# Float32 weights and v for the first five tiles of a windowed attention, in front of two mixture blocks

## The chip, the core and the metric

The kernel runs on one core of a Trainium2 chip. A core has five engines with a queue each, worked through in order: TensorE (PE in the profile, with its weight loads as PEld), VectorE (DVE), ScalarE (ACT), GpSimd (POOL) and SyncE (SP), which here issues every DMA. The metric is the time of one execution on the device, in microseconds (us); lower is better. The median before is 761.0 us (three runs, 760.86 to 761.29).

## The reference

Inputs are float32 or float64; q, k and v have 4 batches, 8 heads, 576 positions and 64 elements a head. The three stages follow each other, and each works on 2304 tokens of 512 elements:

```python
scores = q @ k.T / 8 - slope[h] * abs(i - j)       # kept where 0 <= i - j < 128
attn = exp(scores - max); attn = attn / (sum(attn) + 1e-9)
x = (attn @ v)                                     # heads side by side: 2304 x 512
h = x @ w_in                                       # 512 -> 1024
solu = h * softmax(h); ln = (solu - mean) / sqrt(var + 1e-6) * g_ln
x = ln @ w_out                                     # 1024 -> 512
h = x @ w2_in                                      # 512 -> 2048
g = (a0 + a1 h + a2 h^2 + a3 h^3) / (1 + |b0||h| + |b1|h^2 + 1e-6)
out = g @ w2_out                                   # 2048 -> 512
```

## The kernel before

The tokens are cut into 18 tiles of 128. Because the window is 128 positions, a tile looks at its own keys and at those of the tile before (`nb` = 2 key blocks; tiles 0 and 9 have one). For each tile the program has these steps, each a function that adds operations to a plan: `load` (q, k and v, 256 KB each), `split_v`, `scores`, `attend`, `moe_in` (x @ w_in and the normalisation), `moe_tr` (the transposed result), and for every second tile `moe_out` (@ w_out). After the 18 tiles, `ff_in` and `ff_out` run the last block in groups of 512 tokens. That late part begins at about 340 us.

Precision is bought with splits. A float32 operand is cut into a high and a low part, and three products are added instead of one slow one. The weights of both blocks come as 8-byte numbers: `decode` turns 512 columns into float32 with one ScalarE operation and two VectorE operations (lines 485, 488, 490), and a split follows. `split_w` does this for w_in (eight blocks) and w_out (eight blocks, with `split_scaled`), and both stages of the block wait for it.

In the attention there are two forms of a tile. In a plain tile (`t < PLAIN`, line 366) the exponentials stay float32: ScalarE accumulates their sum, TensorE turns them by products with the identity (line 640), they are copied out of PSUM into `pth` and `ptl`, and `attend_plain` multiplies them by v in float32 (line 698). In all other tiles the exponentials are cut into two float16 parts (`ph` by a copy, `pl` by a subtraction, lines 647 and 648); a transposing DMA on SP's queue turns each part (line 655), two for each half of the heads; v is cut into three parts by two subtractions in `split_v` (lines 571 and 572); and `attend_parts` adds five 16-bit products for each head and key block (line 723). v's sum column gives the sum of the exponentials. Before the change only tile 0 is plain, and `split_v` starts with tile 0, since tile 1 needs tile 0's v in parts.

The order of all work is not written out by hand. Each operation has a priority: the tile's number plus an offset from the table `PR`, plus an offset per stage and engine. `Plan.order` simulates the engines with fixed durations and takes, for every engine that is free, the ready operation of the lowest priority whose buffers are free; the resulting sequence is emitted, and each engine's queue keeps it. A load is an operation of SP in that sequence, so SP too works through loads, transposes and stores in order. Buffers come from small groups of slots (`SLOTS`): six PSUM banks named bk, two q buffers, five k buffers, three v buffers, seven places for raw weights. Where an operation may go to one of several engines (`copy`, `less`), the planner chooses; `copy` from PSUM goes to ScalarE or VectorE only.

TensorE gets zero products (`idle`, line 1014) wherever the planner sees it free before the time `warm` (30 us); their result is read by nobody, and their PSUM bank is kept until then. The planner counts a TensorE operation double before `cold` (6.8 us).

Of the kernel before, what the change touches and what calls it, by code (L numbers as in the profile page):

```python
# [7 lines left out]
F32 = mybir.dt.float32  # L8
# [8 lines left out]
P = 128  # L17
# [3 lines left out]


PR = {
    "bias": -3.854, "biash": -2.053, "load": 4.13, "loadv": 3.0, "v": 1.842, "s": 1.737, "pv": 0.742,
    "win": -0.814, "wout": 0.1, "wstep": 0.43, "tr": 0.53, "mo": 2.078, "e0": 3.42, "e1": 13.032,
    "npre": 26, "plain": 1, "ln": 'dve', "alt.dve": 1500.0, "alt.act": 173.113, "alt.pool": -260.7,
    "ahead": 6.509, "warm": 30000.0, "cold": 6800.0, "last": 0.192, "scores.dve": -0.568,
    "scores.pool": 0.207, "scores.pe": -0.3, "moe_in.dve": 0.919, "attend.act": -0.027,
    "moe_out.pool": 0.104, "scores.act": 0.331, "moe_in.act": 2.226, "attend.dve": 0.049,
    "moe_tr.pe": 0.145, "moe_out.dve": 0.128, "moe_out.act": 0.44, "split_v.dve": 0.115,  # L30
    "moe_out.pe": 0.224, "weights.dve": 0.0, "weights.act": -1.021, "weights.pool": -0.155,
}


# [38 lines left out]
class Plan:  # L73
# [83 lines left out]
    def order(self):  # L157
# [22 lines left out]
        done, now = [], 0.0  # L180
        left = len(self.ops)
        dma = port = 0.0

        held = {}
        for o in self.ops:
# [30 lines left out]
        while left:  # L216
            if not events:
                stuck = [(e, [(o.n, o.pri, [b.group for b in o.allocs]) for o in ready[e]][:4]) for e in engines]
                raise RuntimeError(f"no order: {stuck}")
            now = events[0][0]  # L220
            if self.kept is not None and now >= PR["warm"]:
                self.kept.left -= 1
                if self.kept.slot is not None and not self.kept.left:
                    free[self.kept.slot] = True
                self.kept = None
            while events and events[0][0] <= now:
                _, _, what, o = heapq.heappop(events)
                if what == "ready":
                    for a in o.alts:
                        ready[a[0]].append(o)  # L230
                elif what == "end":
                    for r in {self.where[b.group] for b in o.bufs}:
                        held[r] -= 1
                    for b in o.bufs:
                        b.left -= 1
                        last[b.slot][o.lag and "dma" or o.eng] = now
                        if not b.left:
                            free[b.slot] = True
                            for d in (3.0, 97.0, 127.0, 145.0, 155.0, 200.0, 270.0):
                                heapq.heappush(events, (now + d, seq, "wake", o))  # L240
                                seq += 1
            moved = True
            while moved:
                moved = False
                for e in engines:
                    if busy[e] > now:
                        continue
                    best = None
                    for o in ready[e]:
                        if (best is None or (o.pri, o.n) < (best.pri, best.n)) and fits(o, e) and (  # L250
                                o.alts[0][0] == e or sooner(o, e)):
                            best = o
                    if best is None:
                        if e != "pe" or now >= PR["warm"] or not self.idle:
                            continue
                        best = self.idle(now)
                        if not fits(best, e):
                            continue
                        ready[e].append(best)
                        left += 1  # L260
                        users[best] = ()
                        for r in {self.where[b.group] for b in best.bufs}:
                            held[r] = held.get(r, 0) + 1
                    o = best
                    if e == "pe" and now < PR["cold"] and o.n < len(self.ops):
                        o.alts = tuple((e, 2 * ns, *x) for e, ns, *x in o.alts)
                    for a in o.alts:
                        ready[a[0]].remove(o)
                        if a[0] == e:
                            o.eng, o.ns, o.fn, o.port = a  # L270
                    o.allocs = [b for b in o.bufs if b.slot is None]
                    for b in o.allocs:
                        at[b.group] += 1
                        for s, make in self.groups[b.group]:
                            if clear(s, e):
                                free[s] = False
                                last[s] = {}
                                b.slot, b.make = s, make
                                break
                    o.start = now  # L280
                    if o.lag:
                        busy[e] = now + 460.0
                        dma = max(dma, now + 1100.0) + o.ns
                        o.end = dma + o.lag
                    else:
                        at_port = max(now, port) if o.port else now
                        busy[e] = o.end = at_port + o.ns
                        if o.port:
                            port = o.end
                    done.append(o)  # L290
                    left -= 1
                    moved = True
                    heapq.heappush(events, (o.end, seq, "end", o))
                    seq += 1
                    if busy[e] < o.end:
                        heapq.heappush(events, (busy[e], seq, "free", o))
                        seq += 1
                    for u in users.get(o, ()):
                        wait[u] -= 1
                        if not wait[u]:  # L300
                            t = max(d.end + self.hop(d, u) for d in u.deps)
                            heapq.heappush(events, (max(t, now), seq, "ready", u))
                            seq += 1
# [10 lines left out]
def t_pe(n, cols, wide=True):  # L314

    return n * (cols * 0.4167 + ((17.0 if cols > 256 else 13.3) if wide else 4.0))


def t_act(n, psum=False, ptrs=0):
    return n * 0.833 + (52.0 if psum else 94.0) + 93.0 * ptrs  # L320
# [16 lines left out]
def kernel(  # L337
# [64 lines left out]
    for where, tab in SLOTS.items():  # L402
# [12 lines left out]

    nc.scalar.preload_act_table_set("natural_log_exp_and_others")
    ident = const.tile([P, P], F32, name="ident")
    nc.gpsimd.memset(ident, 0.0)
    nc.gpsimd.affine_select(
        out=ident, in_=ident, compare_op=ALU.not_equal, fill=1.0, base=0,  # L420
        pattern=[[-1, P]], channel_multiplier=1,
    )
    gsb = const.tile([P, KF], F32, name="gsb")
    acoef = const.tile([P, 4], F32, name="acoef")
    bcoef = const.tile([P, 2], F32, name="bcoef")
# [68 lines left out]
    def split(x, xa, ha, la, hk, lk, n, pri, first="pool"):  # L494
        copy(ha, xa, n, [x], [hk], pri)
        less(la, xa, lambda: ha().bitcast(F32), n, [x, hk], [lk], pri, first=first)

    def split_scaled(x, ha, la, hk, lk, g, pri):
# [4 lines left out]
            out=la(), in0=x.t, scalar=g(), in1=ha().bitcast(F32), op0=ALU.mult, op1=ALU.subtract),  # L503
            r=["gsb", x, hk], w=[lk], pri=pri, port=True)

    def split_w(g, pri):
        raw = Buf("wraw", [P, 512, 2], I32)
        x = Buf("wx", [P, 512], F32)
        if g < 2 * KD:
            n, kk = divmod(g, KD)  # L510
            cols = slice(n * 512, n * 512 + 512)
            src = w_in.rearrange("(k p) (f w) -> p k f w", p=P, w=2)[:, kk, cols]
        else:
            f = g - 2 * KD
            src = w_out.rearrange("(k p) (f w) -> p k f w", p=P, w=2)[:, f]
        plan.op("sp", t_dma(P * 4096, 4096), lambda: nc.sync.dma_start(out=raw.t, in_=src),
                w=[raw], pri=pri, lag=LAG)
        decode(x, lambda: x.t, raw, lambda: raw.t, 512, pri)
        if g < 2 * KD:
            split(x, lambda: x.t, lambda: wih[:, kk, cols], lambda: wil[:, kk, cols], ("wih", kk, n),  # L520
                  ("wil", kk, n), 512, pri, first="dve")
        else:
            split_scaled(x, lambda: woh[:, f], lambda: wol[:, f], ("woh", f), ("wol", f),
                         lambda: gsb[:, f:f + 1], pri)


    q_f, k_f, v_f, v_t, pt, ssum, xs = {}, {}, {}, {}, {}, {}, {}
# [483 lines left out]
    b.left = 1  # L1011

    def idle(now):
        return plan.filler("pe", t_pe(1, 256) * (2 if now < PR["cold"] else 1), lambda: nc.tensor.matmul(  # L1014
            b[:, 0:256], still[:, 0:P], still, start=True, stop=True), b)

    plan.idle, plan.kept = idle, b
# [38 lines left out]
```

## Time and profile before

| what | us |
|---|---|
| median of 3 runs | 761.0 |
| the profiled execution, its own time | 762.12 |
| its span, first to last instruction | 760.3 |
| TensorE busy | 738.5 (97%) |
| VectorE busy | 603.3 (79%) |
| ScalarE busy | 480.1 (63%) |
| GpSimd busy | 330.3 (43%) |

The profile is of one execution. Busy time is a sum over instructions; a matmul's record includes its way through the array, so matmuls overlap and TensorE's busy time counts the union. A row of the chain of waits has a start, a length and what the time went to: the chain is followed back from the last event, and a piece of TensorE work on it is as long as the engine needed to get on. For back-to-back matmuls the chain's lengths are therefore the price of one, and the records' own durations are not.

### The profile page before, as it was taken

How to read it: one execution, taken by the hardware profiler on the slowest of the kernel's cores; microseconds unless marked ns; L12 is line 12 of the kernel's file. 1: busy time of each engine (PE TensorE's matmuls, PEld its weight loads, DVE VectorE, ACT ScalarE, POOL GpSimd, SP SyncE). 2: the span in 40 equal slices, each digit the busy share in tenths (PEclk: the TensorE clock that was granted, in tenths of full speed). 3: DMA queues.
4: the chain of work that ended last, by engine and by line, in shares of the span. 5: the costliest groups of instructions: out<-in, count | busy, mean ns of one | idle time of the engine just before them, and what ended most of it. 6: DMA issues, size and time to landing. Idle time of an engine off the chain costs nothing.

```text
span 760.3 us, 14468 instructions
## 1 busy us (share of the span) xinstructions
PE 738.5 (97%) x5369; PEld 631.8 (83%) x5369; DVE 603.3 (79%) x1279; ACT 480.1 (63%) x922; POOL 330.3 (43%) x330
## 2 busy tenths in 40 slices
PE   8968999999999999999999999999999999999997
PEld 7857899898898999989788888888888888888885
DVE  5998987888889757555799988878877788778983
ACT  8666565666576554355887775556765667567782
POOL 5435744443444625036995743334333343323331
PEclk9969999999999999999999999999999999999999
DMA  9996997999998917054541230000100001000010
GB/s 315 276 226 108 194 263 188 238 275 249 245 258 186 177 50 120 28 183 163 160 118 56 84 104 1 1 0 22 56 1 1 1 0 56 0 2 1 1 56 28
DMA packets 123670, 85.36 MB, mean 112 GB/s; under 512 B 74448, under 2 KB 106192, under 8 KB 123600
## 3 DMA queue, kind: packets, MB, share of 16 engines
q1 hardware_dynamic: 123600, 84.44, 43.5%
q8 instruction: 42, 0.69, 0.4%
q14 instruction: 28, 0.23, 0.1%
HBM read 50.86 MB, written 16.25 MB: 88 GB/s over the span
## 4 chain that ended last, share of the span: by engine, by line
PE 85%; DVE 6%; ACT 3%; DMA 3%; issue 2%; SPq 0%; POOL 0%; DVEq 0%; ACTq 0%; POOLq 0%
PE bk L896 23%; PE h L953 14%; PE bk L818 12%; PE h L743 12%; PE bk L953 11%; PE bk L723 4%; PE bk L602 4%; PE bk L578 3%; PE bk L1014 2%; DMA dx<-w2i 1%; DVE bk L930 1%; DMA qn<-in_q_dram 1%; DVE bk L919 1%; DMA pth<-ph 1%; DVE s L617 1%
## 5 line engine op out<-in xcount | busy, mean ns | idle before, releaser
L896 PE MATMUL bk<-yh,wb 128*128 128x512 f32 (+1 forms) x540 | 132.5, 371 | 0.2 <-DVE tcc L928 0.2
L896 PEld LDWEIGHTS bk<-yh,wb 128*128 128x128 f32 x540 | 96.8, 188 | 21.2 <-DVE tcc L928 0.4
L469 POOL TENSOR_TENSOR gl<-tcc,gh 128x512 fp32r<-128x512 f32 x60 | 78.7, 1312 | 75.7 <-ACT gh L457 41.2
L916 ACT ACTIVATE bk<-bk,bcoef 128x512 f32<-128x512 f32 (+1 forms) x80 | 49.5, 618 | 88.5 <-PE bk L896 87.3
L896 PE MATMUL bk<-yh,wa 128*128 128x512 f32 (+1 forms) x420 | 101.8, 371 | 2.0 <-ACT wa L457 0.9
L919 DVE SCALAR_TENSOR_TENSOR bk<-tb,nb,bk 128x512 f32<-128x512 f32 (+1 forms) x80 | 55.9, 699 | 44.6 <-ACT tb L918 43.1
L896 PEld LDWEIGHTS bk<-yh,wa 128*128 128x128 f32 x420 | 75.4, 188 | 18.4 <-DVE tcc L928 1.9
L953 PE MATMUL h<-wo,gh 128*128 128x512 f32 x276 | 84.4, 393 | 0.6 <-ACT gh L457 0.4
L818 PE MATMUL bk<-lh,woh 128*128 128x256 f32 x288 | 84.3, 293 | 0.2 <-DVE ll L801 0.2
L818 PE MATMUL bk<-ll,woh 128*128 128x256 f32 x288 | 81.4, 283 | 0.0
L818 PE MATMUL bk<-lh,wol 128*128 128x256 f32 x288 | 81.4, 283 | 0.0
L469 POOL TENSOR_TENSOR pl<-s,ph 128x512 f16<-128x512 f32 (+1 forms) x58 | 70.1, 1220 | 17.1 <-ACT ph L457 16.1
L953 PE MATMUL bk<-wo,gh 128*128 128x512 f32 x240 | 75.1, 394 | 0.0
L459 POOL TENSOR_SCALAR gh<-tcc 128x512 fp32r<-128x512 f32 (+1 forms) x43 | 26.8, 622 | 106.8 <-DVE tcc L934 105.7
L624 ACT ACTIVATE s<-s,nm 128x256 f32<-128x256 f32 (+1 forms) x144 | 61.9, 487 | 13.3 <-DVE nm L617 13.1
L930 DVE SCALAR_TENSOR_TENSOR bk<-bk,qc,tb 128x512 f32<-128x512 f32 (+1 forms) x80 | 56.3, 704 | 7.3 <-ACT tb L923 5.4
L921 ACT ACTIVATE tb<-bk,qc 128x512 f32<-128x512 f32 (+1 forms) x80 | 51.8, 647 | 14.6 <-DVE bk L919 14.1
L953 PEld LDWEIGHTS h<-wo,gh 128*128 128x128 f32 x276 | 50.7, 188 | 11.5 <-POOL gh L459 0.6
L459 POOL TENSOR_SCALAR ph<-s 128x512 f16<-128x512 f32 (+1 forms) x32 | 20.9, 659 | 90.6 <-DMA pth<-ph 39.1
L924 ACT ACTIVATE tcc<-bk,acoef 128x512 f32<-128x512 f32 (+1 forms) x80 | 59.4, 743 | 0.0
L617 DVE CUSTOM_DVE_ANT_0 s<-bk,bias 128x256 f32<-128x256 f32 (+1 forms) x144 | 51.0, 402 | 9.2 <-PE bk L602 6.1
L928 DVE SCALAR_TENSOR_TENSOR tcc<-tcc,acoef,bk 128x512 f32<-128x512 f32 (+1 forms) x80 | 55.4, 692 | 2.3
(166 smaller groups left out, 1920.9 us busy)
## 6 DMA issues: line engine op xcount, KB each, us to landing
rw<-in_moe_w_in_dram SPq DMA_DIRECT2D x17, 512.0 KB, 4.9
rw<-in_moe_w_out_dram SPq DMA_DIRECT2D x15, 512.0 KB, 5.3
kn<-in_k_dram SPq DMA_DIRECT2D x18, 256.0 KB, 4.9
qn<-in_q_dram SPq DMA_DIRECT2D x18, 256.0 KB, 3.9
vv<-in_v_dram SPq DMA_DIRECT2D x18, 256.0 KB, 5.2
yT<-ys SPq DMA_DIRECT2D x18, 256.0 KB, 2.9
yr<-yT SPq DMA_DIRECT2D x16, 256.0 KB, 3.6
w2i<-dc SPq DMA_DIRECT2D x14, 256.0 KB, 3.4
```

What stands on the lines that cost most here:

```text
L469: "pool": (t_pool(n), lambda: nc.gpsimd.tensor_tensor(out(), a(), b(), op), True),
L617: nc.vector.tensor_tensor_reduce(out=s[:, jj, 0:W], in0=sc[r][:, jj, 0:W], in1=bs, scale=-scale, scalar=3e38, op0=ALU.add, op1=ALU.min, ac ...
L624: nc.scalar.activation(out=s[:, jj, 0:W], in_=s[:, jj, 0:W], func=ACTF.Exp, scale=-1.0, bias=nm[:, h:h + 1], accum_out=sm[:, h:h + 1] if p ...
L743: nc.tensor.matmul(h[:, cols], a[:, kk], w[:, kk, cols], start=(i == 0 and kk == 0), stop=(i == 2 and kk == KD - 1))
L818: nc.tensor.matmul(y[:, r], w[:, f, cols], x[:, f % 4], start=(f == 0 and n == 0), stop=(f == KF - 1 and n == 2))
L896: nc.tensor.matmul(h(), w[:, a, kk], y[:, b, kk, 0:n], start=(i == 0 and kk == 0), stop=(i == 2 and kk == KD - 1))
L919: o("dve", t_dve(n) + 60, lambda: stt(out=A(), in0=R(), scalar=nb1, in1=A(), op0=ALU.mult, op1=ALU.subtract), [bR], [bA])
L921: o("act", t_act(n, True, ptrs=1), lambda: act(out=R(), in_=A(), func=ACTF.Ln, scale=-1.0, bias=qc), [bA], [bR])
L924: o("act", t_act(n, True, 2), lambda: act(out=C(), in_=h(), func=ACTF.Identity, scale=acoef[:, 3:4], bias=acoef[:, 2:3]), [hb, "coef"], [bC])
L928: o("dve", t_dve(n) + 60, lambda: stt(out=C(), in0=C(), scalar=acoef[:, 1:2], in1=h(), op0=ALU.add, op1=ALU.mult), [hb], [bC])
L930: o("dve", t_dve(n) + 60, lambda: stt(out=A(), in0=A(), scalar=qc, in1=R(), op0=ALU.subtract, op1=ALU.mult), [bR], [bA])
L953: nc.tensor.matmul(acc[g][s][2](), a(slice(s * P, (s + 1) * P)), w[:, c], start=(f == 0 and i == 0), stop=(f == KF2 - 1 and i == 2))
```

## The change

`PLAIN` becomes 5, so tiles 0 to 4 are plain: no float16 parts, no transposing DMAs, no split of v for tiles 0 to 3, but sums on ScalarE, turns on TensorE, copies out of PSUM and float32 products. The first block of w_in (`pein` = 1) gets its low part from TensorE: a product with the identity, minus a product of the high part, and a copy out of PSUM. (`peout` = 0: the same for w_out is written but not used.) A constant `minus` is made on VectorE at the start. Zero products are planned until 60 us and no longer counted double. The planner takes TensorE to be slow for 6.8 us after any wait of over 3 us, by a factor of 1.85. Most priorities change a little: among others v is loaded earlier (4.28 tiles ahead, 3.0 before), q and k later (3.432, 4.13 before), and 28 blocks of the last stage's weights, not 26, are decoded ahead into DRAM.

```diff
-    "npre": 26, "plain": 1, "ln": 'dve', ...
+    "npre": 28, "plain": 5, "ln": 'dve', ...
-    "ahead": 6.509, "warm": 30000.0, "cold": 6800.0, "last": 0.192, ...
+    "ahead": 6.6, "warm": 60000.0, "cold": 6800.0, "pein": 1, "peout": 0, "last": 0.169,
...
+        slow = PR["cold"]
...
-                    if e == "pe" and now < PR["cold"] and o.n < len(self.ops):
-                        o.alts = tuple((e, 2 * ns, *x) for e, ns, *x in o.alts)
+                    if e == "pe":
+                        if now - busy[e] > 3000.0:
+                            slow = now + PR["cold"]
+                        if now < slow and o.n < len(self.ops):
+                            o.alts = tuple((e, 1.85 * ns, *x) for e, ns, *x in o.alts)
...
+    minus = const.tile([P, P], F32R, name="minus")
...
+    nc.vector.tensor_scalar(minus, ident, -1.0, None, ALU.mult)
...
+    def lower(x, w, ha, la, hk, lk, r, pri):
+
+        d = Buf("bk", [P, 512], F32)
+
+        def mm():
+            nc.tensor.matmul(d.t, w(), x.t, start=True, stop=False)
+            nc.tensor.matmul(d.t, minus, ha(), start=False, stop=True)
+        plan.op("pe", 1085.0, mm, r=[x, hk] + r, w=[d], pri=pri)
+        copy(la, lambda: d.t, 512, [d], [lk], pri, psum=True)
...
+            if g < PR["pein"]:
+                copy(part[0], lambda: x.t, 512, [x], [part[2]], pri)
+                lower(x, lambda: ident, *part, [], pri)
+            else:
+                split(x, lambda: x.t, *part, 512, pri, first="dve")
...
-        return plan.filler("pe", t_pe(1, 256) * (2 if now < PR["cold"] else 1), lambda: nc.tensor.matmul(
+        return plan.filler("pe", t_pe(1, 256), lambda: nc.tensor.matmul(
```

## Rows read from the trace of the kernel before

**Rows 1.** By stage: stretch, length, busy us per engine, clock, DMA share, GB/s.
```profile
0.00:34.00 34.00, 30.67 (x309) 26.13 (x309) 25.22 (x77) 23.18 (x58) 18.10 (x23) 0.95 0.93 288
34.00:60.00 26.00, 19.16 (x131) 15.03 (x132) 24.61 (x61) 16.54 (x33) 7.46 (x8) 0.74 0.86 221
60.00:83.00 23.00, 19.89 (x278) 17.05 (x276) 19.66 (x69) 16.81 (x36) 14.18 (x14) 1.00 0.89 162
83.00:340.00 257.00, 255.48 (x2729) 232.24 (x2725) 197.20 (x564) 147.20 (x311) 106.59 (x103) 1.00 0.80 186
340.00:740.00 400.00, 397.97 (x1860) 328.81 (x1860) 329.32 (x497) 270.49 (x473) 181.60 (x181) 1.00 0.13 44
740.00:760.30 20.30, 15.37 (x75) 12.58 (x73) 7.30 (x17) 5.83 (x15) 2.36 (x4) 0.97 0.07 26
```

**Rows 2.** Groups of TensorE instructions: count, busy us, mean ns, idle before.
```profile
L1014 PE MATMUL bk<-still 128*128 128x256 bf16 x145 | 18.7, 292 | 1.1 <-DVE still L429 1.1
```

**Rows 3.** The chain of waits, 4 to 16 us: start, length, work.
```profile
7.64 1.83 PE bk L602 x16
9.47 1.47 PE bk L640 x6
...
11.87 1.09 PE bk L602 x16
12.96 1.03 PE bk L698 x8
...
14.10 0.84 PE bk L698 x8
```

**Rows 4.** The chain of waits, 86 to 125 us.
```profile
87.35 5.50 PE h L743 x24
...
97.04 1.31 PE bk L578 x12
```

**Rows 5.** The same table by stage, for 8 to 11 us.
```profile
8.00:11.00 3.00, 3.00 (x23) 2.64 (x21) 1.47 (x8) 2.02 (x10) 2.50 (x3) 0.50 1.09 376
```

**Rows 6.** The chain of waits, 24 to 62 us.
```profile
31.68 1.34 PE bk L723 x40
...
34.18 1.19 PE h L743 x4
...
50.68 2.04 PE bk L602 x14
...
54.45 6.11 PE h L743 x16
```

**Rows 7.** SP's queue in order of time: start, length, DMA issued.
```profile
37.08 4.01 SPq L655 DMA_TRANSPOSE ptl<-pl  x1
```

**Rows 8.** VectorE in order of time: start, length, operation [idle before].
```profile
11.61 1.51 DVE L468 TENSOR_TENSOR v<-v1r 128x512 bf16<-128x512 f32 x1 [0.70 <-POOL v1r L469]
...
14.48 2.23 DVE L488 TENSOR_SCALAR dc<-dc 128x512 int32<-128x512 int32 x2
...
26.93 0.41 DVE L488 TENSOR_SCALAR dc<-dc 128x512 int32<-128x512 int32 x1
...
30.26 1.46 DVE L468 TENSOR_TENSOR wil<-dc,wih 128x512 fp32r<-128x512 f32 x1
31.64 0.68 DVE L701 TENSOR_TENSOR xr<-bk,st 128x512 f32<-128x512 f32 x1
```

**Rows 9.** GpSimd in order of time, 8 to 90 us.
```profile
13.98 2.45 POOL L469 TENSOR_TENSOR pl<-s,ph 128x512 f16<-128x512 f32 x2
```

**Rows 10.** Groups of ScalarE instructions, 0 to 60 us.
```profile
L624 ACT ACTIVATION_READ_ACCUMULATOR s<-s,nm 128x1 f32 x8 | 1.5, 187 | 0.0
...
L457 ACT ACTIVATE xh<-bk 128x512 fp32r<-128x512 f32 x2 | 1.2, 597 | 3.7 <-PE bk L578 3.7
```

**Rows 11.** The same table by stage, for 10 to 60 us.
```profile
10.00:60.00 50.00, 42.60 (x390) 35.60 (x389) 46.97 (x113) 32.70 (x65) 22.26 (x21) 0.85 0.92 262
```

**Rows 12.** TensorE in order of time, 4 to 16 us.
```profile
4.87 1.16 PE L602 MATMUL bk<-kn,qn 64*128 64x128 f32 x16
```

More of the change, by code (lines that the diff above doesn't have):

```diff
@@ L23 @@
 PR = {
[L24 to L31, printed above, removed]
+    "bias": -3.938, "biash": -2.341, "load": 3.432, "loadv": 4.28, "v": 1.842, "s": 1.737, "pv": 0.742,
+    "win": -0.911, "wout": 0.1, "wstep": 0.43, "tr": -0.387, "mo": 2.066, "e0": 3.613, "e1": 12.889,
+    "npre": 28, "plain": 5, "ln": 'dve', "alt.dve": 1500.0, "alt.act": 173.113, "alt.pool": -260.7,
+    "ahead": 6.6, "warm": 60000.0, "cold": 6800.0, "pein": 1, "peout": 0, "last": 0.169,
+    "scores.dve": -0.59, "scores.pool": 0.107, "scores.pe": -0.3, "moe_in.dve": 0.919,
+    "attend.act": -0.139, "moe_out.pool": 0.132, "scores.act": 0.331, "moe_in.act": 2.097,
+    "attend.dve": 0.165, "moe_tr.pe": -0.433, "moe_out.dve": -0.69, "moe_out.act": -0.295,
+    "split_v.dve": 0.115, "moe_out.pe": 0.224, "weights.dve": 0.16, "weights.act": -0.915,
+    "weights.pool": -0.155,
 }
@@ L417 @@
     ident = const.tile([P, P], F32, name="ident")
+    minus = const.tile([P, P], F32R, name="minus")
+    diag = const.tile([P, PR["peout"], P], F32, name="diag") if PR["peout"] else None
     nc.gpsimd.memset(ident, 0.0)
@@ L519, in split_w @@
         if g < 2 * KD:
-            split(x, lambda: x.t, lambda: wih[:, kk, cols], lambda: wil[:, kk, cols], ("wih", kk, n),
-                  ("wil", kk, n), 512, pri, first="dve")
-        else:
-            split_scaled(x, lambda: woh[:, f], lambda: wol[:, f], ("woh", f), ("wol", f),
-                         lambda: gsb[:, f:f + 1], pri)
+            part = (lambda: wih[:, kk, cols], lambda: wil[:, kk, cols], ("wih", kk, n), ("wil", kk, n))
+            if g < PR["pein"]:
[3 more added lines that the diff above has]
+                split(x, lambda: x.t, *part, 512, pri, first="dve")
+        else:
+            part = (lambda: woh[:, f], lambda: wol[:, f], ("woh", f), ("wol", f))
+            gain = lambda: gsb[:, f:f + 1]
+            if f < PR["peout"]:
+                plan.op("pool", 250, lambda: nc.gpsimd.tensor_scalar(
+                    diag[:, f], ident, gain(), None, ALU.mult), r=["gsb"], w=[("diag", f)], pri=PR["bias"] + 0.01 * f)
+                plan.op("act", t_act(512, ptrs=1), lambda: nc.scalar.activation(
+                    out=part[0](), in_=x.t, func=ACTF.Identity, scale=gain()), r=["gsb", x], w=[part[2]], pri=pri)
+                lower(x, lambda: diag[:, f], *part, [("diag", f)], pri)
+            else:
+                split_scaled(x, *part, gain, pri)
     q_f, k_f, v_f, v_t, pt, ssum, xs = {}, {}, {}, {}, {}, {}, {}
```

## The prediction, before the result was known

> **What bounds the kernel now.** I read the busy table by stage first. TensorE is busy all the time from 83 us to 740 us (255.5 of 257 us, then 398.0 of 400) at a granted clock of 1.00; before 83 us it is not, and VectorE is the full one there (24.6 of 26 us in 34 to 60) [rows 1]. So the kernel is a TensorE-bound run behind a start in which TensorE waits for VectorE. The end moves only if the start loses less TensorE time, or if TensorE gets more or less to do. I therefore keep an account of TensorE's lost time:
>
> - Idle: 3.3 + 6.8 + 3.1 = 13.3 us before 83 us, and 1.5 + 2.0 + 4.9 = 8.5 us after it [rows 1].
> - Zero products of line 1014, which only fill waits: 18.7 us, all early [rows 2].
> - Work at the lower clock. Tile 1's first scores took 1.83 us where 1.09 is the price, and six turns took 1.47 where 6 x 0.109 = 0.65 is (1.31 us for 12) [rows 3, 4]. The clock granted in 8 to 11 us was 0.50 [rows 5]. After the hole at 45 us, 14 score products took 2.04 us instead of 14 x 0.068 = 0.95 and 16 moe products 6.11 instead of 16 x 0.229 = 3.67 (5.50 us for 24) [rows 4, 6]. Together 0.74 + 0.82 + 1.09 + 2.44 = 5.1 us.
>
> Early loss: 13.3 + 18.7 + 5.1 = 37.1 us. Real work at full clock: 760.3 - 37.1 - 8.5 = 714.7 us. The change must be weighed as added work against early loss removed.
>
> **What is added on TensorE.** Tiles 1 to 4 change their kind; tile 0 was plain already, so its rows are the prices. Its eight float32 products of weights and v took 1.03 + 0.84 = 1.87 us [rows 3], or 0.234 each; a tile with two key blocks has 16 of them, 3.74 us. Turning its weights takes 16 transposes of 128x128 at 0.109 us [rows 4], 1.75 us. Removed are the two halves of 40 16-bit products, 1.34 us each [rows 6], 2.68 us. Net 3.74 + 1.75 - 2.68 = 2.81 us a tile, 11.2 us for four. The low part of the first w_in block ("lower") is one float32 and one float32r product of 512 columns. The float32r one costs 0.23 us; no row has the float32 one at 512 columns, so I bound it by two float32r products (0.46 us) and by 4 x 2 x 0.109 = 0.87 us from the turns; its gain on VectorE is one subtraction. I take the upper end, 1.0 to 1.1 us in all, and use 1.0. Sum: 12.2 us of new work.
>
> **What is removed elsewhere.** (a) Sixteen transposing DMAs (four a tile) leave SP's queue. One of them occupied it for 4.01 us, from 37.1 us on [rows 7], with all later loads behind it; tile 1's second half waited for that landing. (b) Sixteen subtractions of low weight halves and eight that split v go, most of them GpSimd's, a few VectorE's. One of VectorE's, 1.51 us at 11.6 us, stood in front of tile 1's second scores [rows 8]. (c) VectorE runs slower beside GpSimd: two integer shifts took 2.23 us beside two GpSimd subtractions (2.45 us) where one takes 0.41 alone, and a subtraction of 512 elements 1.46 us where a product of that size took 0.68 [rows 8, 9]. With (b), that stretch goes too: 1.4 + 0.8 us in these two places, and 1.5 for the moved v split, 3.7 us that I can name before tile 0's output is scaled at 31.64 us [rows 8].
>
> **What is added elsewhere.** ScalarE takes four copies of a turned 512-element block per tile (0.60 us each) and eight accumulator reads (0.187 us each, partly overlapped), and loses up to four 0.6 us copies of the high weights that GpSimd shared: +1.5 to +3.9 us a tile, 6 to 16 us for four [rows 10]. It was busy 32.7 us of 50 in 10 to 60 us [rows 11], so 39 to 48. That hides it at the low end only; I take 8, since tiles 3 and 4 finish late in that stretch. VectorE's new constant ("minus") waits at the start for GpSimd's identity and holds back the zero products' operand: 0 to 0.5 us of an interval in which nothing real runs; I take 0. The first v load moves ahead of the first k and q: 0 to 0.6 us; I take 0.1 and let the start stay 4.9 us, where the first scores begin now [rows 12]. The buffers of v are now held until the next tile's products; the third stays in its slot for about one tile: 0 to 1 us, taken at 0, because v 3 is not needed before tile 3. The fill block keeps one of six PSUM banks until 60 us of planned time and not 30: 0 to 3 us, taken at 1 inside the waits below. Two more early w2 decodes and the new priorities after 83 us lie under a full TensorE: -1 to +1 us, taken at 0. Fewer or more zero products cost nothing where TensorE would wait; one in the way costs its 0.11 us.
>
> **The new loss.** First products: 4.9 us in. The first moe products began at 34.2 us [rows 6], 2.5 us behind the scaling at 31.64. With 3.7 us named and some more from shifts and loads further on, I put them at 29 us (bounds 24 and 34). Until then TensorE has these to do: tile 0 (0.6 scores, 0.9 turns, 1.9 products, 0.4), tile 1 (2.2 + 1.75 + 3.74 + 0.4), tile 2's scores and turns (4.0) and the low part (1.0): 16.9 us in the 24.1 us from 4.9 to 29, a loss of 7.2. After that the old kernel lost 6.8 + 3.1 us idle from 34 us and 3.5 at the low clock. The second moe block came only at 54.45 us [rows 6]: between the two lay the DMA landing, the hole and the low clock. Those causes are removed, but VectorE still has the w_out decoding; I keep a third, 4.4 us, and 0.4 for the early clock. New loss: 4.9 + 7.2 + 4.4 + 0.4 = 16.9 us.
>
> Span: 714.7 + 12.2 + 8.5 + 16.9 = 752.3 us. The profiled execution took 762.12 us, 1.8 over its span; the median shown is 761.0, 0.7 over this span, so I forecast 753.0 us on the scale of the medians.
>
> **A rule against it.** Twelve turns in a row at 97 us ran at 0.109 us each, amid a stretch with a granted clock of 1.00 [rows 1, 4]; but the six turns at 9.5 us ran inside a stretch at 0.50 [rows 3, 5]. The change brings 64 more turns into the start. The Trainium skill (TensorE: Matmul & The Clock Gate, Part 4: PE-mode transpose) says that transposes do not count as activity for the full clock, which would speak against the change. The late row disagrees for short bursts among other products; the early row cannot tell turns from the wait before them. As a mechanism of this kernel it is the fourth rival.
>
> **The rivals.**
> 1. ScalarE takes VectorE's place (ends slower). Each turned block must be copied out by ScalarE before a product can start; at its upper bound (48 of 50 us) the start stays as long as now. Tiles 1 and 2 and the low part still fit where the zero products are, but tiles 3 and 4 fall behind the point at which TensorE is full: 2 x 2.81 = 5.6 us, so 761.0 + 5.6 = 766.6. It decides once ScalarE is over 95% busy between 10 and 50 us. For it: its sum; against it: 17 us free now.
> 2. A wash. The early loss falls by no more than the 12.2 us of work that is put in, to 24.9: 761.0. So it would be if the new work only replaces zero products, and moe starts at 34 us as now. For it: the 18.7 us of fill; against it: the DMA and GpSimd waits that go.
> 3. A deep gain. Moe starts at 24 us and nothing waits after it: loss 4.9 + 2.2 + 0.4 = 7.5 us, 743.6. For it: TensorE has more than enough ready once tile 1 is plain; against it: eight w_in decodes on VectorE must be done first.
> 4. Low clock from 5 to 29 us: 16.9 us of work take as much again, less the 7.2 free: +9.7, 762.7.
>
> **How the numbers follow.** Forecast (loss 11 to 23 us, 747 to 759): 0.63. Rival 1: 0.09. Rival 2: 0.10 (0.02 faster, 0.07 same, 0.01 slower). Rival 3: 0.14. Rival 4: 0.04. So faster by over 0.2% (under 759.5, about what a measurement of this kernel can tell from no change) 0.63 + 0.14 + 0.02 = 0.79, within it 0.07, slower 0.01 + 0.09 + 0.04 = 0.14. The range goes from 746, leaving out most of rival 3, to 761.5, taking in rival 2 and leaving out the two slower ones.
>
> **What would show it.** Right: first moe products before 31 us and the second block before 45; no granted clock under 0.9 in 15 to 80 us; fill plus idle before 83 us near 17 us; TensorE full from about 45 us; VectorE's shifts at 0.41 us. Float32 products at 0.117 us an instruction, turns at 0.11. Wrong: moe starting at 34 us (rival 2), ScalarE full (rival 1), turns at 0.25 us (rival 4), or a loss after 83 us well over 8.5 us, which would mean that the new order pays elsewhere.

## The result

The changed kernel takes 751.5 us (median of four runs, 750.94 to 753.49) where the kernel before took 761.1 beside it: a ratio of 0.987 (95% interval 0.985 to 0.990). The forecast was 753.0 us in a range of 746 to 761.5. The profiled execution has a span of 749.1 us.

The table by stage, which answers to [rows 1], has the same columns.

```profile
0.00:34.00 34.00, 32.19 (x288) 26.91 (x288) 23.67 (x89) 26.93 (x80) 9.55 (x16) 1.00 0.89 294
34.00:60.00 26.00, 26.00 (x208) 22.97 (x208) 24.53 (x63) 23.92 (x65) 5.33 (x4) 1.00 0.50 163
60.00:83.00 23.00, 23.00 (x209) 20.82 (x210) 21.53 (x70) 17.28 (x37) 12.46 (x13) 1.00 0.63 147
83.00:340.00 257.00, 256.28 (x2648) 231.95 (x2647) 190.70 (x548) 147.20 (x307) 100.80 (x99) 1.00 0.78 193
340.00:740.00 400.00, 398.16 (x1843) 328.73 (x1842) 331.05 (x499) 268.76 (x474) 169.72 (x171) 1.00 0.11 36
740.00:749.10 9.10, 3.92 (x18) 2.88 (x16) 0.69 (x1) 0.60 (x1) 0.00 (x0) 1.00 0.15 58
```

TensorE was idle for 13.3 us before 83 us; now it is idle for 1.8, nearly all of it before its first instruction. The granted clock, 0.95 and 0.74 in the first two stages before, is 1.00 in all rows. (That column does not show the very start: in 1.7 to 4 us, 11 zero products took 2.2 us, in 6 to 8 us, 20 took 2.0, both with a clock of 1.00.) After 83 us the picture is as it was. ScalarE is the engine that changed most: 26.9 and 23.9 us in the first two stages, 23.2 and 16.5 before; GpSimd's work there falls from 18.1 and 7.5 to 9.6 and 5.3.

The chain of waits shows what fills the start. It answers to [rows 6] and [rows 4], with line 773 for 743, 728 for 698, 670 for 640 and 753 for 723.

```profile
24.84 0.93 PE h L773 x4
...
27.76 1.93 PE bk L728 x16
...
35.19 1.14 PE h L773 x4
...
39.50 1.73 PE bk L728 x16
...
43.08 0.44 PE bk L670 x4
...
51.71 5.75 PE h L773 x24
57.46 1.75 PE bk L670 x16
```

Tile 0's moe products come in two halves now, the second from 35.2 to 39 us, since the second half of w_in is decoded late. The second tile's start only at 51.7 us; it was 54.45 us [rows 6]. In between stand the turns and the attention products of tiles 2 and 3 and the scores of tile 4 (tile 1's products came before, tile 4's come at 62.8 and 71.4 us): that is what replaced waits, zero products and slow work.

```profile
65.40 5.53 PE h L773 x24
...
75.06 1.34 PE bk L753 x40
...
79.36 5.50 PE h L773 x24
...
96.95 5.50 PE h L773 x24
```

The third tile's moe products begin at 65.15 us in the order of time; they began at 72.84. The fourth tile's begin at 79.4 us, those of the fifth at 96.95; 87.35 us was the fourth's start before [rows 4]. So 8 us of the 11.2 us between the two profiled spans are there at 79 us; of the rest 0.8 us is less idle time after 83 us [rows 1], and what remains is work that stands earlier now.

### The profile page after: what moved, and what is told of

It reads as the page before. It is cut to its first block, busy times and chain, and to the rows that moved or that the text cites. A ratio compares the mean times of both kernels' runs of the same rounds, so it can differ in the third digit from the quotient of the medians.

```text
span 749.1 us, 14112 instructions
## 1 busy us (share of the span) xinstructions
PE 739.6 (99%) x5205; PEld 634.3 (85%) x5205; DVE 592.2 (79%) x1266; ACT 484.7 (65%) x960; POOL 297.9 (40%) x302
## 4 chain that ended last, share of the span: by engine, by line
PE 89%; DVE 5%; ACT 4%; DMA 1%; issue 1%; SPq 0%; POOL 0%; POOLq 0%; DVEq 0%
PE bk L926 24%; PE h L983 14%; PE h L773 13%; PE bk L848 13%; PE bk L983 11%; PE bk L632 4%; PE bk L753 4%; PE bk L608 3%; PE bk L1044 1%; PE bk L728 1%; ACT s L654 1%; DMA dx<-w2i 1%; DVE bk L960 1%; PE bk L670 1%; DVE bk L949 1%
## 5 line engine op out<-in xcount | busy, mean ns | idle before, releaser
L926 PEld LDWEIGHTS bk<-yh,wa 128*128 128x128 f32 x420 | 75.4, 188 | 18.1 <-DVE tcc L958 1.9
L654 ACT ACTIVATE s<-s,nm 128x256 f32<-128x256 f32 (+1 forms) x144 | 63.9, 488 | 14.3 <-DVE nm L647 14.0
L467 POOL TENSOR_SCALAR gh<-tcc 128x512 fp32r<-128x512 f32 (+1 forms) x39 | 24.2, 622 | 105.2 <-DVE tcc L964 104.5
L951 ACT ACTIVATE tb<-bk,qc 128x512 f32<-128x512 f32 (+1 forms) x80 | 51.7, 647 | 12.6 <-DVE bk L949 12.0
L647 DVE CUSTOM_DVE_ANT_0 s<-bk,bias 128x256 f32<-128x256 f32 (+1 forms) x144 | 51.0, 404 | 10.5 <-PE bk L632 8.8
L958 DVE SCALAR_TENSOR_TENSOR tcc<-tcc,acoef,bk 128x512 f32<-128x512 f32 (+1 forms) x80 | 55.4, 692 | 2.1
L964 DVE SCALAR_TENSOR_TENSOR tcc<-tcc,acoef,bk 128x512 f32<-128x512 f32 (+1 forms) x80 | 55.4, 693 | 2.1
L848 PEld LDWEIGHTS bk<-lh,woh 128*128 128x128 f32 x288 | 55.0, 191 | 1.1
```

Source lines behind the costliest of these rows:

```text
L654: nc.scalar.activation(out=s[:, jj, 0:W], in_=s[:, jj, 0:W], func=ACTF.Exp, scale=-1.0, bias=nm[:, h:h + 1], accum_out=sm[:, h:h + 1] if p ...
L848: nc.tensor.matmul(y[:, r], w[:, f, cols], x[:, f % 4], start=(f == 0 and n == 0), stop=(f == KF - 1 and n == 2))
L926: nc.tensor.matmul(h(), w[:, a, kk], y[:, b, kk, 0:n], start=(i == 0 and kk == 0), stop=(i == 2 and kk == KD - 1))
L951: o("act", t_act(n, True, ptrs=1), lambda: act(out=R(), in_=A(), func=ACTF.Ln, scale=-1.0, bias=qc), [bA], [bR])
L958: o("dve", t_dve(n) + 60, lambda: stt(out=C(), in0=C(), scalar=acoef[:, 1:2], in1=h(), op0=ALU.add, op1=ALU.mult), [hb], [bC])
L964: o("dve", t_dve(n) + 60, lambda: stt(out=C(), in0=C(), scalar=acoef[:, 0:1], in1=A(), op0=ALU.add, op1=ALU.mult), [bA], [bC])
```

## The experiments

Each group of four ran on one chip beside the kernel before, in five rounds. The time is the median; the ratio is to the kernel before on that chip, with its 95% interval. Between groups I compare ratios: 0.001 is 0.76 us.

**One plain tile.** The change without its main part.

```diff
-    "npre": 28, "plain": 5,
+    "npre": 28, "plain": 1,
```

> The changed kernel with one plain tile instead of five; the zero products until 60 us, the new priorities, the low part of one w_in block on TensorE and everything else stay. Theory (the plain tiles are what pays, since they take float16 parts, splits of v and transposing DMAs out of the start): the gain of 9.6 us goes, 758 to 764 us, first moe products after 29 us, idle before 83 us above 6 us. Rival (the new order and the longer zero products pay, and the plain tiles are only carried along): 755 us or less, since 11 us of added TensorE work go too.

764.5 us, ratio 1.004 (1.003 to 1.005): slower than before by a little, and some 13 us slower than with five. The rival falls. TensorE issues 285 zero products where the changed kernel issues 106, and the second moe block comes 7 us later. The account closes: 179 zero products more (some 19.5 us) and 5.5 us more idle time, against some 10.5 us less work, make 14.5 of the 15.2 us between the profiled spans. The sign of 6 us of idle time before 83 us failed: it was 4.0, since zero products stand in the waits. These are a group's row (count, busy us, mean ns) and two rows of TensorE in order of time:

```profile
L1044 PE MATMUL bk<-still 128*128 128x256 bf16 x285 | 36.2, 284 | 1.8 <-DVE still L437 1.8
```

```profile
30.36 1.16 PE L773 MATMUL h<-wih,xh 128*128 128x512 f32 x4
...
58.66 2.11 PE L773 MATMUL h<-wih,xh 128*128 128x512 f32 x8
```

**Five plain tiles in the kernel before.**

```diff
-    "npre": 26, "plain": 1,
+    "npre": 26, "plain": 5,
```

> The kernel before with five plain tiles and nothing else changed: old priorities, zero products until 30 us, no low part on TensorE. Theory (plain tiles pay by themselves): 750 to 756 us, first moe products before 28 us. Rival (the order and the longer zero products pay): 759 us or more, since 11 us of TensorE work are added.

758.5 us, ratio 0.994 (0.991 to 0.996), with runs from 753.2 to 760.1. That lies between the two: plain tiles pay by themselves, but the median is over the theory's 756. The profiled run, near the low end, shows what is missing. Its first moe products start at 25.3 us, and 34 to 60 us has 24.7 us of TensorE work; but ahead of tile 3's moe products the chain runs into VectorE, which decodes weights (line 490) between the steps that free tile 2's moe result (lines 751 and 758):

```profile
71.10 0.45 PE bk L578 x4
...
72.81 1.21 DVE st L751
74.03 1.39 DVE dc L490
...
76.46 0.59 DVE dc L490
...
78.93 6.18 PE h L743 x19
```

TensorE's table there (stretch, length, busy us per engine, granted clock):

```profile
72.00:78.00 6.00, 2.40 (x35) 2.04 (x32) 5.80 (x7) 3.10 (x6) 3.71 (x4) 1.00 0.85 179
78.00:83.00 5.00, 4.43 (x15) 3.35 (x14) 5.00 (x21) 3.20 (x6) 0.54 (x1) 0.66 1.42 290
```

One hole of some 3.6 us and the low clock behind it: as I read it, the old priorities place VectorE's decoding badly for a start that has become shorter.

**The changed kernel with fewer zero products,** in the same order of real work.

```diff
+            zeros.append(1)
+            if len(zeros) <= 41:
+                nc.tensor.matmul(b[:, 0:256], still[:, 0:P], still, start=True, stop=True)
```

> The changed kernel in the same order of all real work, but of its 106 zero products only the first 41 (before the first scores) are issued; the 65 later ones are left out. Theory (zero products only fill waits that ScalarE and VectorE make, 65 x 0.11 = 7.1 us of them): the time stays at 751 to 752 us, TensorE is idle some 7 us more, and the granted clock stays at 1.00 because the holes are short. Rival (the zero products hold the clock up, and the longer warm stretch is part of the gain): the granted clock falls to 0.5 somewhere between 9 and 45 us and the time rises to 754 us or more.

750.8 us, 0.985 (0.983 to 0.987), the span 749.0. Without 65 zero products the time does not rise and the clock stays up, though 64 more turns than before the change run in this start. They only fill waits.

```profile
0.00:34.00 34.00, 30.52 (x242) 23.65 (x242) 22.49 (x85) 25.61 (x77) 9.04 (x16) 1.00 0.90 304
34.00:60.00 26.00, 24.48 (x192) 21.55 (x190) 24.84 (x67) 24.11 (x66) 5.60 (x5) 1.00 0.47 150
```

**Thirteen fewer of the opening ones,** the same edit with `not 28 < len(zeros) <= 41`.

> The changed kernel in the same order, but 13 of the 41 zero products ahead of the first scores are left out. The 41 took TensorE from 1.76 to 7.96 us, at 0.151 us each. If they stand in the way of scores whose q and k have landed, the scores begin 1 us or more earlier, ScalarE's full stretch begins earlier with them, and the time falls by about 1 us, to 750.5 us. Rival (q and k land at about 8 us anyway, or the clock comes up later without them): no change, or up to 1 us more.

751.3 us, 0.986 (0.984 to 0.988): no change that can be told. The 28 took 0.20 us each, the 41 of the kernel above 0.18, since the first of them run slowly, and not equally long in every execution (the changed kernel's 41 took 6.2 us in its profiled run, these 7.5). So the scores came 0.6 us before the changed kernel's 7.89, and 1.9 before those of the run above, whose span is 1.4 us shorter all the same: the times of these runs do not tell what a later first product costs. (Two traces further down show one that was kept.) TensorE in order of time, first with 28, then with 41:

```profile
1.77 5.64 PE L1049 MATMUL bk<-still 128*128 128x256 bf16 x28 [1.77 <-DVE still L437]
7.33 1.16 PE L632 MATMUL bk<-kn,qn 64*128 64x128 f32 x16
```

```profile
1.77 7.52 PE L1049 MATMUL bk<-still 128*128 128x256 bf16 x41 [1.77 <-DVE still L437]
9.21 1.16 PE L632 MATMUL bk<-kn,qn 64*128 64x128 f32 x16
```

**Three plain tiles** (`"plain": 3`).

> The changed kernel with three plain tiles. Theory (each plain tile takes waits out of the start, and the four together moved the time from 764.5 to 751.5 us): tiles 3 and 4 pay too, so 754 to 760 us. Rival (tiles 3 and 4 lie where TensorE is full, as it is from about 10 us on, and only cost their 2.7 us each): 746 to 750 us.

759.5 us, 0.997 (0.996 to 0.999): with tiles 3 and 4 in parts the kernel is 8 us slower. TensorE is busy 19.5 us of 23 in 60 to 83 us, at a clock of 0.85, and waits there for VectorE (1.8 and 1.1 us) and GpSimd (0.5); a transposing DMA costs 0.8 us after 83 us. As an account: 53 zero products more than with five (some 5.8 us), 6.0 us more idle time (4.2 of it before 83 us) and the lower clock, against some 5.3 us less work. Holes of this kind also come with other changes of the order (below), so how much of the 8 us the two tiles are worth by themselves is not shown.

```profile
L1044 PE MATMUL bk<-still 128*128 128x256 bf16 x159 | 22.3, 291 | 1.8 <-DVE still L437 1.8
```

**Seven plain tiles** (`"plain": 7`):

> The changed kernel with seven plain tiles. Theory (plain pays only while TensorE has waits to fill, and tiles 5 and 6 come after 60 us, where it has none): 2 x 2.7 us more, 755 to 759 us. Rival (every tile without splits and transposing DMAs frees more than it costs): 751 us or less.

757.0 us, 0.995 (0.994 to 0.996): 5.5 us more than with five by the medians, 5.7 by the ratios, 2.8 a tile. The start is the same, zero products and idle time too (107 against 106, 9.8 us in all against 9.5), so no new hole is in the comparison: work is added where TensorE is full.

```profile
L1044 PE MATMUL bk<-still 128*128 128x256 bf16 x107 | 16.5, 292 | 1.8 <-DVE still L437 1.8
```

**High copies on GpSimd,** to relieve ScalarE.

```diff
-                split(x, lambda: x.t, *part, 512, pri, first="dve")
+                copy(part[0], lambda: x.t, 512, [x], [part[2]], pri, first="pool")
+                less(part[1], lambda: x.t, lambda: part[0]().bitcast(F32), 512, [x, part[2]], [part[3]], pri, first="dve")
```

> The changed kernel with GpSimd, not ScalarE, as first choice for the high copies of seven w_in blocks; four of eight were ScalarE's, 0.6 us each. Theory (ScalarE, busy 38.1 us of 40 between 10 and 50 us, is what now holds the start): 2 us less, 749 to 750 us. Rival (VectorE holds it just as much, and slows beside GpSimd): 751 to 755 us.

755.9 us, 0.992 (0.990 to 0.993). As slow as the rival said and a little more, but not for its reason: the start is as full as before, and the loss lies after 83 us, in one wait of the last block's first products for GpSimd (a table row, and a row of TensorE's waits: total us, times, longest):

```profile
34.00:60.00 26.00, 26.00 (x218) 22.98 (x218) 23.71 (x67) 24.88 (x68) 6.55 (x6) 1.00 0.48 155
...
83.00:340.00 257.00, 252.60 (x2611) 229.08 (x2611) 194.93 (x559) 146.04 (x305) 101.00 (x98) 0.99 0.75 191
```

```profile
PE bk L927 <- POOL wa L467: 3.3, 1, 3.3
```

So this run does not tell whether ScalarE or VectorE holds the start.

**The old loads' order** and **no low part on TensorE.**

```diff
-    "load": 3.432, "loadv": 4.28,
+    "load": 4.13, "loadv": 3.0,
```

> The changed kernel with the old priorities of the loads (k and q 4.13 tiles ahead, v 3.0). Theory (the loads' order is not what pays): 750 to 754 us; the first scores come near 5 us and not at 7.9, and the w_in loads about 1.4 us later. Rival (the five plain tiles alone gave 758.5 us because of the old loads): 756 us or more.

758.3 us, 0.995 (0.994 to 0.996), which the theory missed. The first scores came at 7.2, not near 5, since the zero products are in front of them; the start is full, and again one hole follows, ahead of the third moe block:

```profile
60.00:83.00 23.00, 19.28 (x180) 16.80 (x177) 21.80 (x64) 15.23 (x31) 11.98 (x11) 0.94 0.72 166
```

```profile
PE h L773 <- DVE st L798: 3.5, 1, 3.5
```

The other is `"pein": 0`:

> The changed kernel without the low part of the first w_in block on TensorE: one subtraction more on VectorE (0.7 us), a copy less on ScalarE (0.6 us), 1.1 us less TensorE work. Theory (it is a small term): 750.5 to 752.5 us. Rival (it frees VectorE where the first moe products wait for it): 753 us or more, and those products start 0.7 us or more after 21.7 us.

756.3 us, 0.992 (0.990 to 0.993). Both signs of the rival are there: the first moe products start 1.1 us later. But 34 to 83 us stays full of TensorE work (49.0 of 49), and the time is lost after 83 us: 252.9 us busy of 257, with waits for GpSimd and ScalarE at the last block's weights. So the reason is neither's. Each such edit makes the planner write another order, and by the ratios another order cost 3 to 6 us here, in one or two holes.

**30 products of zeros added,** to the kernel with 41 zero products, at 18 us or at 68 us (there the same loop stands in tile 2's moe products), without any change of order. The edit for 18 us:

```diff
             nc.tensor.matmul(d.t, w(), x.t, start=True, stop=False)
+            for _ in range(30):
+                nc.tensor.matmul(d[:, 0:256], still[:, 0:P], still, start=False, stop=False)
```

> The changed kernel's order with only the first 41 zero products (that kernel took 750.8 us), and 30 products of zeros, 3.3 us of TensorE time, added to the sum of the low part at about 18 us. Theory (there TensorE waits for ScalarE and VectorE, so work put on it is hidden): 750.3 to 752 us. Rival (TensorE bounds the start as well, and the added float32 products are paid in full and only outweighed): 753.5 us or more.

> The same kernel with the 30 products of zeros added to tile 2's moe products at about 68 us instead. Theory (from about 60 us on TensorE is what everything waits for): 3.0 to 3.6 us more than with 41 zero products alone, 754 us. Rival (later waits still take some of it up): 752.5 us or less.

Early: 752.1 us, 0.988 (0.986 to 0.989), an interval that overlaps that of the kernel without them (0.983 to 0.987); 1.9 us more by the ratios, 0.8 less by the profiled spans. Late: 753.3 us, 0.990 (0.989 to 0.992), clear of it: 3.8 us more by the ratios, 1.9 by the spans, for 3.3 us of work. The late half of the theory stands. For the early half the times leave it open, but the traces say more, one execution each, as the three kernels have one order. The first scores came at 9.21 us without the 30 products, at 7.71 and 7.66 in these two, because the opening zero products happened to run faster. These are the starts of the third tile's moe products, without, early and late:

```profile
65.85 2.08 PE L773 MATMUL h<-wih,xh 128*128 128x512 f32 x8
```

```profile
64.99 2.07 PE L775 MATMUL h<-wih,xh 128*128 128x512 f32 x8
```

```profile
64.17 2.07 PE L773 MATMUL h<-wih,xh 128*128 128x512 f32 x8
```

In the late run nothing is added up to there, and it is 1.7 us ahead: the earlier opening of 1.55 us is kept in full. In the early run 0.9 of 1.5 us is left, so the 30 products had cost 0.6 us of their 3.3 by then. The fifth tile's moe products start at 97.38, 96.51 and 98.99 us: the early ones still cost 0.6 us, the late ones now 3.3, all of it. So in these executions most of the early work is hidden. The early run's profiled execution is the fastest of its four, though (750.1 us; the others 752.1 to 752.4), and what the others lost no trace shows.

**Zero products until 60 us in the kernel before** (`"warm": 60000.0`).

> The kernel before with zero products until 60 us of planned time instead of 30, nothing else. Theory (they only fill waits; they can at most keep the clock up over the hole at 45 us, whose slow work cost 3.5 us): 757 to 761 us. Rival (the fill is what pays): 754 us or less.

766.9 us, 1.009 (1.007 to 1.011): outside what either side expected. The clock is at 1.00 through the start, 61 zero products stand where the hole was, and the second moe block starts at 54.6 us, as before. So the low clock alone was not what delayed it (though this, too, is another order). The loss lies in new holes: 4.5 us of idle time in 60 to 83 us and 5.2 in 83 to 340.

```profile
34.00:60.00 26.00, 25.35 (x215) 20.90 (x215) 24.81 (x65) 19.04 (x39) 8.47 (x8) 1.00 0.86 213
```

```profile
42.06 6.76 PE bk L1014 x61
...
54.64 5.79 PE h L743 x24
```

## Why the prediction was right

**Added work.** Right. A half's eight products (16 instructions) took 1.73 us in most cases (1.93 at 27.8 us) and four turns 0.44: 3.46 + 1.75 us a tile against 2.46 to 2.68 of parts, so 2.5 to 2.75 (predicted 2.81). The low part took 1.1 us from 17.6 to 18.7 us, the upper end chosen for the float32 product.

```profile
1.76 6.20 PE L1044 MATMUL bk<-still 128*128 128x256 bf16 x41 [1.76 <-DVE still L437]
7.89 1.16 PE L632 MATMUL bk<-kn,qn 64*128 64x128 f32 x16
...
17.60 1.02 PE L519 MATMUL bk<-dc,ident 128*128 128x512 f32 x2
18.06 0.80 PE L520 MATMUL bk<-wih,minus 128*128 128x512 f32 x1
...
21.66 1.18 PE L773 MATMUL h<-wih,xh 128*128 128x512 f32 x4
```

One price in the prediction's list of what TensorE can do meanwhile was too low: tile 0's scores are 16 instructions at 0.068 us, 1.1 us and not 0.6. The account closes: opening zero products 6.2 us, 65 others at 0.11 us 7.15, idle 1.8 + 7.7, so real work is 749.1 - 22.9 = 726.2 us; predicted were 714.7 + 12.2 = 726.9.

**Early loss.** 1.8 + 13.4 = 15.2 us against 16.9, near partly by luck. The first scores came at 7.9, not 4.9 us: I had passed over what the new price of a zero product does, 41 of them ahead of the scores, slow at first. So the opening cost 8.0 us where the sum has 4.9. Between it and the first moe products 28 zero products took 3.1 us where the sum has 7.2; the 37 behind them took 4.1, where it has 4.4. The two large errors cancel. Of the low clock nothing is left but the slow opening.

**Where the gain arises.** The first moe products came at 21.7 us, under my bounds of 24 and 34; but the sign "second block before 45 us" failed: it came at 51.7, 3 us earlier than before. I had taken the gain to be moe blocks that move forward. The first block's lead of 12.5 us shrinks to 2.7 at the second and is 7.7 at the third. What happened is that TensorE did the attention of tiles 1 to 3, and of tile 4 around the third block, while w_in and w_out were still decoded; from the second on the blocks follow each other without the waits of [rows 1]. The runs with one, three, five and seven plain tiles (764.5, 759.5, 751.5, 757.0 us) show both sides: plain tiles pay while their attention falls into the wait, and cost 2.8 us each behind it. They were tested in pairs; at which number between three and seven the gain turns into a loss is not shown.

**What is removed.** VectorE runs at its own pace, mostly: an integer shift takes 0.43 us where a pair took 2.23 [rows 8]; of 15 shifts before 60 us, 11 take 0.42 to 0.43, and four that lie beside GpSimd's subtractions 1.0 to 1.5. Tile 0's output is scaled at 17.0 us, not 31.6. The 3.7 us that I had named do not explain that, and the step from them to the first moe products at 29 us was wrong: before, seven of VectorE's operations of line 490 stood ahead of the scaling, now two of the same kind (line 498) do. It comes with the plain tiles: with five of them in the old order the scaling is at 15.4 us, with one and the new priorities at 26.6. The last low part of w_in comes at 33.5 us, only 2 us earlier than before.

```profile
14.66 0.43 DVE L496 TENSOR_SCALAR dc<-dc 128x512 int32<-128x512 int32 x1
...
17.04 0.69 DVE L731 TENSOR_TENSOR xr<-bk,st 128x512 f32<-128x512 f32 x1
...
33.50 0.69 DVE L476 TENSOR_TENSOR wil<-dc,wih 128x512 fp32r<-128x512 f32 x1
```

**The rivals.** The first had a point from which it decides, ScalarE over 95% busy in 10 to 50 us. The point was reached, 38.14 of 40 us, and the rival did not come: a full ScalarE held TensorE up little. In the run without 65 zero products TensorE waited for it 0.9, 0.6, 0.3 and 0.2 us before 62 us. The criterion was wrong; the bounds behind it (39 to 48 us of 50, 10 to 60 us) were right, with 46.1. That is 13.4 us more, where I had taken 8, a number that went into no term of the sum.

```profile
10.00:50.00 40.00, 39.95 (x372) 35.02 (x368) 36.59 (x111) 38.14 (x107) 10.71 (x9) 1.00 0.82 276
```

The wash was too pessimistic, the deep gain too hopeful: moe did start before 24 us, but the first zero products and the wait for w_in's second half kept 15 us of loss. The clock rival is refuted: the granted clock stays at 1.00 in its stretch, and 16 turns in a row took 1.75 us, 0.109 each, at 57.5 us with a granted clock of 1.00 around them, also where 65 zero products were left out. The sentence of the Trainium skill that transposes do not count as activity for the full clock (TensorE: Matmul & The Clock Gate, Part 4: PE-mode transpose) is not borne out by these runs, in which turns always stand among other products; what turns alone would do no run here shows.

**After 83 us** the loss was 7.7 us, 8.5 predicted: nothing pays or costs there. That this took a fitting order was not in the prediction; the runs with another order lost 3 to 6 us, most of it in one or two holes after 60 us, and five plain tiles with the old priorities gained only part.

**Open.** Which of the removed pieces (transposing DMAs, subtractions on GpSimd, subtractions on VectorE) the old waits were due to, as no run takes out one alone. What relieving ScalarE or VectorE would give now: the changed kernel's chain of waits runs mostly through ScalarE from 9.1 to 24.1 us and through VectorE from 44.8 to 51.7, where VectorE comes to tile 0's moe result (line 788) only behind the decoding of w_out, so each has its stretch, but no run shows the price.

```profile
9.09 2.42 ACT s L654 x12
...
22.00 0.67 ACT dc L493
...
46.06 2.11 DVE wol L510 x2
...
50.49 1.13 DVE u L788
```

And how much of the 5 to 7 us between five plain tiles in the old order and the changed kernel belongs to the loads, the low part or the other priorities, as each edit changes the whole order. Leaving out 65 zero products gave 750.8 us, which the intervals don't tell from the changed kernel, so no version is shown to beat it.

## What to carry to other kernels

Where a start is bound by the engines that prepare operands, move work from them to the engine that waits, even at a higher price per item, as long as the item falls into the wait; count the items, for those behind the wait cost their full difference (here 2.8 us each). Look for the gain in what the waiting engine can do meanwhile, not only in when the blocked step starts. And where a planner writes the order, test a part by leaving it out in the same order if you can: a changed parameter is a new order, and that alone was worth 3 to 6 us here.

## What was not expected of the hardware

Filling TensorE's waits until 60 us held the granted clock at 1.00 and bought nothing: the block behind the hole started at 54.6 us instead of 54.45. And the changed kernel kept 1.00 without the fill: in 34 to 60 us TensorE was busy 24.5 of 26 us with waits of at most 0.6 us, while a hole of 3.6 us in another run left a mean of 0.66 in the five microseconds behind it.
